# Three sums of the first groups moved into TensorE, and all order lists rewritten, in a gated linear attention with a maxout layer behind it

## The chip, the cores and the metric

The kernel runs on one core of one Trainium2 chip. A core has a matrix engine (TensorE, PE in the profile), VectorE (DVE), ScalarE (ACT), GpSimd (POOL), a queue engine that issues most transfers (SyncE, SP) and 16 DMA engines. The metric is the device time of one execution in microseconds (us); lower is better. Before the change three runs gave 565.18, 568.17 and 564.65 us; the median is 565.18.

## The reference

The first block is a recurrence with complex decays, for 4 batches x 8 heads, 768 steps, 48 dimensions:

```python
mag = np.sqrt(a_re * a_re + a_im * a_im)
scale = np.minimum(mag, 0.999) / (mag + 1e-06)
a_re_n, a_im_n = (a_re * scale, a_im * scale)
for t in range(S):
    ar, ai = (a_re_n[:, :, t, :, None], a_im_n[:, :, t, :, None])
    new_re = ar * S_re - ai * S_im
    new_im = ar * S_im + ai * S_re
    kv = np.einsum('bhd,bhe->bhde', k[:, :, t], v[:, :, t])
    S_re, S_im = (new_re + kv, new_im)
    y[:, :, t] = np.einsum('bhd,bhde->bhe', q[:, :, t], S_re)
```

Its output, as 3072 tokens of 384 features, goes through a maxout layer with weights in 64-bit floats (w1 to w3 of 384x768, w_out of 768x384):

```python
h = np.maximum(np.maximum(x @ w1, x @ w2), x @ w3)
return (h @ w_out).astype(np.float32)
```

## The kernel before

The steps are cut into 12 groups (numbers 0 to 11). A group is 128 steps of two batch entries, called x and y; six groups make one pair of batch entries. A decay is kept as the logarithm of its size and as an angle in turns, so that products of decays become sums over steps.

The order of all work is written out by hand as a long text, `SCHEDULE`, of words like `csx:0`: a step's name, x or y where it is done for one entry, and the group. A trailing 0 or 1 ahead of the colon (`lnw0:0`) means that only one half, x or y, is done. `run` (L952 ff.) turns a word into instructions; the helper class `Bound` chains the instructions of each engine, so each engine keeps the text's order strictly (all instructions therefore carry that helper's line, L209). `SLOTS` deals out the four double banks of PSUM in the order in which they are asked for. `OTHER` lists words that go to VectorE instead of their usual engine. Words that matter:

- `Lr`, `Li`, `Lk`, `Lq`, `Lv`: loads of a_re, a_im, k, q, v, issued on SP.
- `sqr sqi add lnL expw expe`: squares, their sum `L`, its logarithm, the size `w` and its inverse `e`. `relu` (tile `Ln`), `lne` (tile `e`) are the two parts of the logarithm of the decay; `Lnop` adds them: on VectorE in group 0, by an accumulating DMA from GpSimd's queue (`increase`, L254) in most later groups.
- `abs`, `pw` or `addw`: size plus |a_re|; in groups 0 and 1 (`SUMS`) it is summed by TensorE with the identity. `lnw expL mulw mulai stt atan`: the angle's half tangent and its arctangent in `w`. `half`: a_re's sign becomes a half turn in `ar`. `turn`: `w` = -w/pi + ar, on VectorE. `Cd`: the turns of the group before are added to `ar` by small DMAs.
- `cs` (L585 ff.): running sums of turns, by TensorE with the triangle `upto`. `t nf af sa sb`: fraction of a turn, sine and cosine.
- `sums`, `F` (L621 ff.): TensorE sums of `Ln` over ranges of steps, with 0/1 matrices (`mid`, `rest`, `cuts`); `En Ek Eq` and `f0` to `f3` are their exponentials on ScalarE. A factor tile `F` has the 48 dimensions twice, at partitions 0 and 64. `F` computes each head once, for one of the two places, and four instructions `f0` to `f3` write each result to both.
- `mk mq uk uq kEn`, `tpk tpq Kc Qc`, `Q1 Q2 QB KB QG`, `A B g0..g3 b0 b1`: rotated and scaled k and q, their transposes, the scores and their masked copy.
- `dk h0..h3`: the state; `y`, and its copy `x` (`xx`, `xy` in the lists): the attention output as features.
- `U..`/`u..`: up products and running maximum. Group 0 does them in halves (`U01x:0`), later groups whole (`U11:1`, 128x256 matmuls). `S P r o D`: the down product by a scheme with seven products, and the store.
- `WL Wa Wb Wc We Wf Wg`: 12 blocks of weights are loaded as 64-bit floats and turned into 32-bit ones by one ScalarE and four VectorE operations. `Wg` subtracts w1's block from that of w2 or w3, mostly by an accumulating DMA. `T t M m`: a product w1 @ w_out made once.
- `Zf`, `Zg`: zeros in the factor tiles' rows that `f0` to `f3` leave out, and in the state tiles.

Of the kernel before, what the change touches and what calls it, by code (L numbers as in the profile page):

```python
# [26 lines left out]
sqr:1 Wf9:0 half1:0 Lkx:0 csx:0 tx:0 nfx:0 mkx:0 sqi:1 atan1:0 add:1 turn1:0 afx:0 Wb10:0 sax:0 sbx:0 WL11:0 ukx:0
lnL:1 csy:0 Wc10:0 Eqy:0 Eky:0 expe:1 ty:0 Lqy:0 uqx:0 We10:0 Wf10:0 tpkx:0 kEnx:0 Wa11:0 Wb11:0 nfy:0 xor:1 tpqx:0
Qcx:0 T0:0 WL1:0 Wa1:0 Lky:0 Lvx:0 Wc11:0 f3x:0 f0x:0 Wb1:0 f2x:0 Q2x:0 We11:0 QBx:0 Kcx:0 relu:1 expw:1 abs:1
Wf11:0 half:1 Fy:0 f0y:0 T2:0 Lrx:2 lne:1 WL2:0 Lnop:1 Zg:0 pw:1 Wc1:0 Q1x:0 Lix:2 KBx:0 mky:0 t2:0 Lry:2 Ax:0  # L30
Wa2:0 We1:0 Wb2:0 t0:0 g0x:0 lnw:1 expL:1 Cdx:0 f2y:0 f1y:0 f3y:0 sqr:2 afy:0 Wf1:0 Wc2:0 say:0 sby:0 mulw:1
# [10 lines left out]
mqy:1 uqy:1 sumsx:2 Ekx:2 U22y:0 u22y:0 Oy:0 KBx:1 uky:1 tpky:1 sbx:2 afy:2 sax:2 Lkx:2 h0x:1 Eqx:2 mkx:2 h1x:1
h2x:1 Q1x:1 Enx:2 Lvy:1 tpqy:1 oy:0 Lqx:2 h3x:1 Qcy:1 Q2x:1 QBx:1 Ax:1 Kcy:1 QGx:1 Fx:2 f3x:2 Q1y:1 g0x:1 Q2y:1
sumsy:2 U22x:0 f1x:2 f2x:2 Lvx:2 g1x:1 g2x:1 g3x:1 Eqy:2 f0x:2 say:2 Ay:1 Bx:1 b0x:1 u22x:0 Lrx:3 Lry:3 Ox:0 kEny:1
KBy:1 sby:2 b1x:1 h0x:2 ukx:2 sqr:3 add:3 lnL:3 relu:3 expe:3 QBy:1 lne:3 Dy:0 g0y:1 Lnop:3 g1y:1 g2y:1 By:1 ox:0
g3y:1 b1y:1 Lky:2 Lqy:2 mqy:2 uqy:2 Eky:2 Eny:2 Liy:4 yx:1 xx:1 mqx:2 tpkx:2 uqx:2 expw:3 Kcx:2 mky:2 tpqx:2 dky:1
# [5 lines left out]
nfx:3 J4:0 afx:3 P7:1 Ay:2 sbx:3 ty:3 nfy:3 Lvx:3 g0y:2 g1y:2 g2y:2 Lry:4 sqr:4 By:2 sqi:4 add:4 sax:3 lnL:4 expe:4
Liy:5 Lix:5 g3y:2 ukx:3 uqx:3 P1:1 b0y:2 P6:1 dky:2 b1y:2 r1:1 h1y:2 QGy:2 h2y:2 Py:1 Lvy:3 Px:1 P4:1 h3y:2 xor:4
P5:1 lne:4 relu:4 yy:2 expw:4 abs:4 tpqx:3 r6:1 r5:1 r7:1 r57:1 oy:1 tpkx:3 xy:2 afy:3 P2:1 Lky:3 Qcx:3 S4:1 Kcx:3
P3:1 mky:3 half:4 Lnop:4 Fy:3 addw:4 f2y:3 f3y:3 f0y:3 f1y:3 kEnx:3 dkx:3 sumsx:4 ox:1 Lqy:3 mqy:3 Cdy:3 h0x:3
Q1x:3 QBx:3 h1x:3 lnw:4 h2x:3 Lqx:4 h3x:3 KBx:3 QGx:3 Q2x:3 Fx:4 Lkx:4 expL:4 Ekx:4 Eqx:4 mqx:4 say:3 sby:3 f1x:4
f2x:4 uqy:3 uky:3 U11:2 u11:2 U01:2 mulw:4 mulai:4 stt:4 f3x:4 mkx:4 Enx:4 u01:2 f0x:4 sqi:5 atan:4 Ax:3 g0x:3
g1x:3 Dy:1 Lry:5 g2x:3 h0y:3 Cdx:3 Bx:3 U02:2 g3x:3 turn:4 b0x:3 Lvy:4 u02:2 tpky:3 kEny:3 b1x:3 Kcy:3 tpqy:3 csx:4
Lrx:5 Qcy:3 tx:4 xor:5 csy:4 ty:4 nfy:4 sqr:5 add:5 Lqy:4 lnL:5 nfx:4 dky:3 relu:5 Q2y:3 sumsy:4 h1y:3 expe:5 afx:4
Eky:4 S3:2 h2y:3 h3y:3 yx:3 Eqy:4 Eny:4 KBy:3 Q1y:3 QBy:3 U12:2 Dx:1 u12:2 S1:2 expw:5 abs:5 addw:5 xx:3 P7:2 P1:2  # L60
sbx:4 half:5 sax:4 lne:5 Ay:3 g0y:3 By:3 Cdx:4 P5:2 r1:2 ukx:4 lnw:5 g1y:3 S2:2 S4:2 QGy:3 g2y:3 g3y:3 Py:2 Cdy:4
Lvx:4 h0x:4 P4:2 uqx:4 expL:5 afy:4 say:4 P6:2 b1y:3 Px:2 P2:2 P3:2 tpkx:4 r6:2 r5:2 r7:2 Liy:6 r57:2 tpqx:4
mulai:5 mqy:4 Lrx:6 b0y:3 yy:3 Kcx:4 KBx:4 Lix:6 sby:4 ox:2 mulw:5 Qcx:4 oy:2 stt:5 xy:3 Q1x:4 QBx:4 Lnop:5 sumsx:5
kEnx:4 Lky:4 mky:4 uky:4 QGx:4 Lry:6 Ekx:5 Fy:4 U01:3 U11:3 f0y:4 f1y:4 sqi:6 Enx:5 sqr:6 Lqx:5 u01:3 add:6 lnL:6
Q2x:4 relu:6 expe:6 u11:3 Lkx:5 Lvy:5 mkx:5 f2y:4 f3y:4 uqy:4 h0y:4 Eqx:5 mqx:5 U02:3 atan:5 dkx:4 u02:3 Fx:5 h1x:4
h2x:4 h3x:4 f0x:5 f1x:5 turn:5 Ax:4 g0x:4 g1x:4 g2x:4 g3x:4 f3x:5 f2x:5 xor:6 Bx:4 b1x:4 b0x:4 Dx:2 U12:3 u12:3
# [5 lines left out]
f3y:5 h0y:5 mulai:6 stt:6 QBx:5 u01:4 Eqx:6 U11:4 Q2x:5 half:6 Lrx:7 Enx:6 Ekx:6 tpky:5 tpqy:5 Qcy:5 u11:4 kEny:5
Lkx:6 Ax:5 sqi:7 atan:6 Kcy:5 mqx:6 mkx:6 g0x:5 Q2y:5 g1x:5 g2x:5 Bx:5 g3x:5 turn:6 b0x:5 Lvy:6 b1x:5 U02:4 u02:4
h0x:5 Lry:7 sqr:7 U12:4 add:7 lnL:7 u12:4 Fx:6 f2x:6 f0x:6 f3x:6 f1x:6 dkx:5 h1x:5 dky:5 sumsy:6 S3:4 csx:6 Eqy:6
Dx:3 h1y:5 KBy:5 Eny:6 expe:7 Lqy:6 mqy:6 Q1y:5 QBy:5 csy:6 ty:6 nfy:6 tx:6 relu:7 expw:7 nfx:6 P7:4 P1:4 Eky:6
lne:7 afx:6 By:5 yx:5 Ay:5 xor:7 S1:4 g0y:5 afy:6 P5:4 say:6 sbx:6 S2:4 g1y:5 g2y:5 xx:5 sax:6 uqx:6 g3y:5 Py:4
P4:4 r1:4 ukx:6 S4:4 P6:4 b1y:5 Dy:3 sby:6 b0y:5 Px:4 P2:4 P3:4 tpkx:6 abs:7 Kcx:6 tpqx:6 Lky:6 Qcx:6 QGy:5 r6:4
r5:4 r7:4 r57:4 ox:4 yy:5 xy:5 Lnop:7 sumsx:7 Fy:6 f0y:6 uqy:6 mky:6 uky:6 f2y:6 Lvx:6 Q1x:6 QBx:6 f3y:6 addw:7
lnw:7 Lix:8 U01:5 f1y:6 oy:4 kEnx:6 KBx:6 Ekx:7 u01:5 QGx:6 dkx:6 Lrx:8 Q2x:6 h1x:6 h2x:6 expL:7 Lry:8 Eqx:7 h3x:6
half:7 Lkx:7 mkx:7 Lqx:7 mulai:7 Ax:6 sqr:8 mulw:7 mqx:7 Cdy:6 stt:7 Cdx:6 U11:5 Liy:8 sqi:8 u11:5 atan:7 add:8  # L80
# [959 lines left out]
```

## Time and profile before

| | |
|---|---|
| median of 3 runs | 565.18 us |
| profiled execution | 564.54 us |
| its span (first to last instruction) | 562.9 us |
| mean granted TensorE clock | 0.981 |
| TensorE busy | 527.2 us (94%) |
| VectorE busy | 483.1 us (86%) |
| ScalarE busy | 393.6 us (70%), 73.1 of it in 57 table loads |
| GpSimd busy | 74.7 us (13%) |

The profile is one execution. Busy time counts an engine's instructions, not waits. `PE` is matmuls, `PEld` weight loads, which overlap them; each matmul in 32-bit floats leaves two records. A busy TensorE need not be at its peak. An arrow `<-` in brackets names what ended the idle time before an instruction. In the time lines a row's length may reach over the start of the next row, as instructions overlap a little; the distance from start to start is what an instruction costs its engine in a full queue.

### The profile page before, as it was taken

The numbers are of one execution on the slowest core, as the hardware profiler recorded it, in microseconds if no ns is written. First come the engines' busy times: TensorE is split into PE (matmuls) and PEld (weight loads), VectorE is DVE, ScalarE is ACT, GpSimd is POOL, SyncE is SP. The second block draws the span as 40 slices with busy tenths as digits, with TensorE's granted clock in tenths as the row PEclk, the third lists the DMA queues.
The fourth block names the chain that finished last, engine by engine and source line by source line (L and its number), as shares of the span: only waits on it lengthen the run. The fifth ranks groups of instructions, "written<-read, shape, count | busy, mean of one in ns | idle before, by whom it ended". The sixth has DMA issues, their size and how long they took to land.

```text
span 562.9 us, 22756 instructions
## 1 busy us (share of the span) xinstructions
PE 527.2 (94%) x10086; PEld 450.3 (80%) x10086; DVE 483.1 (86%) x762; ACT 393.6 (70%) x673; POOL 74.7 (13%) x115
## 2 busy tenths in 40 slices
PE   1579779989999999999999999999999999999997
PEld 0355578768888898888888988888888988998886
DVE  5996997999999998999897999989997799996423
ACT  6996986897679988775967776977787856631100
POOL 8304241002020020010002002002101102000000
PEclk9959899999999999999999999999999999999999
DMA  8987985463443432175353352352362233000000
GB/s 224 269 207 174 174 164 94 84 122 63 72 84 69 81 58 52 38 135 107 60 90 83 62 92 51 75 95 54 58 133 37 43 65 71 4 30 2 2 29 28
DMA packets 142097, 48.30 MB, mean 86 GB/s; under 512 B 130480, under 2 KB 135472, under 8 KB 142000
## 3 DMA queue, kind: packets, MB, share of 16 engines
q1 hardware_dynamic: 136128, 37.77, 31.5%
q0 software_dynamic: 5872, 9.08, 9.4%
q8 instruction: 79, 1.29, 0.9%
q14 instruction: 18, 0.15, 0.1%
HBM read 33.03 MB, written 4.72 MB: 67 GB/s over the span
## 4 chain that ended last, share of the span: by engine, by line
PE 74%; ACT 9%; DMA 6%; DVE 5%; issue 5%; SPq 1%; POOL 0%; ACTq 0%; DVEq 0%; POOLq 0%
PE up L209 29%; PE op L209 21%; PE y L209 6%; PE A L209 4%; PE tp L209 4%; PE dk L209 3%; PE cs L209 2%; PE sums L209 2%; DMA Ln<-e 2%; DMA w<-w 2%; PE F L209 1%; ACT L L209 1%; ACT xhx L209 1%; ACT e L209 1%; PE B L209 1%
## 5 line engine op out<-in xcount | busy, mean ns | idle before, releaser
L209 PE MATMUL up<-xhx,w 128*128 128x256 f32 x792 | 177.6, 382 | 0.2
L209 PEld LDWEIGHTS up<-xhx,w 128*128 128x128 f32 x792 | 148.4, 190 | 21.8 <-issue 0.9
L209 ACT ACT_TABLE_LOAD x57 | 73.1, 1283 | 1.8 <-PEq L1024 0.8
L209 POOL DMA_DIRECT2D ar<-nf x40 | 33.6, 1278 | 129.6 <-DVE ar L209 127.3
L209 PE MATMUL op<-wo,xhx 128*128 128x192 f32 (+1 forms) x220 | 49.0, 363 | 0.7 <-issue 0.5
L209 DVE TENSOR_TENSOR Q<-Q,f 112x1024 f32<-112x1024 f32 (+1 forms) x48 | 45.3, 952 | 0.4 <-ACT Q L209 0.4
L209 ACT COPY atm<-B 32x128 f32<-32x128 f32 x96 | 24.6, 256 | 28.4 <-PE B L209 14.8
L209 DVE TENSOR_TENSOR ot<-ot,op 128x192 f32<-128x192 f32 (+1 forms) x66 | 27.5, 418 | 15.4 <-PE op L209 8.7
L209 PEld LDWEIGHTS op<-wo,xhx 128*128 128x128 f32 x220 | 36.6, 190 | 5.0 <-issue 0.6
L209 PE MATMUL y<-atm,vb 128*32 128x64 f32 x1152 | 38.7, 221 | 0.0
L209 PE MATMUL y<-QG,g 112*32 112x64 f32 x1408 | 37.7, 219 | 0.6 <-ACT g L209 0.6
L209 ACT ACTIVATE f<-F 48x232 f32<-48x232 f32 x96 | 34.4, 359 | 3.5 <-PE F L209 1.6
L209 DVE TENSOR_TENSOR xhx<-xhx,up 128x768 f32<-128x768 f32 x22 | 21.0, 953 | 17.4 <-PE up L209 17.3
L209 PEld LDWEIGHTS y<-atm,vb 128*32 128x32 f32 x1152 | 32.1, 109 | 4.0 <-issue 2.3
L209 PEld LDWEIGHTS y<-QG,g 112*32 112x32 f32 x1408 | 34.6, 109 | 0.7 <-ACT g L209 0.7
L209 PE MATMUL op<-wo,strassen 128*128 128x192 f32 x176 | 33.0, 331 | 0.0
L209 ACT ACTIVATE xhx<-up 128x768 f32<-128x768 f32 x19 | 15.4, 809 | 25.1 <-PE up L209 25.1
L209 DVE COPY_PREDICATED atm<-masko,A 128x256 f32<-128x256 uint8 x72 | 31.3, 434 | 1.5
L209 PE MATMUL op<-w,strassen 128*128 128x192 f32 x176 | 32.4, 330 | 0.0
L209 PE MATMUL A<-Q,K 112*32 112x80 f32 x1536 | 31.4, 234 | 0.5 <-DVE Q L209 0.5
L209 PEld LDWEIGHTS A<-Q,K 112*32 112x32 f32 x1536 | 27.2, 110 | 4.7 <-issue 3.3
L209 POOL DMA_DIRECT2D Ln<-e x9 | 9.2, 1027 | 161.0 <-ACT e L209 112.9
(152 smaller groups left out, 1119.0 us busy)
## 6 DMA issues: line engine op xcount, KB each, us to landing
ar<-in_a_re_dram SPq DMA_DIRECT2D x24, 192.0 KB, 3.3
ai<-in_a_im_dram SPq DMA_DIRECT2D x24, 192.0 KB, 4.8
q<-in_q_dram SPq DMA_DIRECT2D x96, 48.0 KB, 2.7
k<-in_k_dram SPq DMA_DIRECT2D x96, 48.0 KB, 2.7
vb<-in_v_dram SPq DMA_DIRECT2D x96, 48.0 KB, 2.5
out_dram<-ot SPq DMA_DIRECT2D x24, 192.0 KB, 2.9
Ln<-e POOLq DMA_DIRECT2D x9, 384.0 KB, 4.2
w<-L POOLq DMA_DIRECT2D x9, 384.0 KB, 4.6
```

The source lines that it names most:

```text
L209: ins = f(*a, **kw)
```

## The change

Three sums of the first groups are left to TensorE's accumulation, and `SCHEDULE`, `SLOTS` and `OTHER` are replaced as a whole.

- Groups below `TURNS` = 2 have no `turn`: `cs` accumulates two products, `scaled` (the triangle times -1/pi) with the arctangents and `upto` with the half turns.
- Groups below `APART` = 2 have no `Lnop`: `sums` and `F` accumulate over `Ln` and over `e`. Group 0 keeps `e` in the place of the state tile `g3`, which is zeroed later (`Zh`); group 1 has a buffer of its own (`e+`).
- Groups below `WHOLE` = 3 compute `F` for both places, with 64 columns of weights, so one instruction `f0` takes the place of four. The tiles have 16 zero columns behind their end for the last head. `Zf` is gone.
- Group 0 keeps |a_re| in `L`, as the later groups do (`ADDS` is gone).

```diff
-    SUMS, ADDS = 2, 1
+    SUMS, TURNS, APART, WHOLE = 2, 2, 2, 3
...
+    scaled = const.tile([P, P], FP, name="scaled")
...
+        pool.tensor_single_scalar(out=scaled, in_=upto, scalar=-1.0 / math.pi, op=OP.mult)
...
         for nm in "Lwe":
-            once((nm, g), lambda: nat1.tile([P, W], FP, tag=nm, name=nm))
+            n = 16 if nm == "e" and g < APART else 0
+            if n and g == 0 and (nm, g) not in T:
+                T["e+", g] = gs[3].rearrange("p c i d -> p (c i d)")[:, 0:W + n]
+            once((nm + "+", g), lambda: nat1.tile([P, W + n], FP, tag=nm + "+" if n else nm, name=nm))
+            if n and (nm, g) not in T:
+                pool.memset(T["e+", g][:, W:], 0.0)
+            T[nm, g] = T[nm + "+", g][:, 0:W]
...
         elif name == "Lnop":
-            if g >= ADDS:
-                increase(part("Ln"), e)
-            else:
-                dve.scalar_tensor_tensor(out=part("Ln"), in0=L, scalar=-LNMAX, in1=e, op0=OP.add, op1=OP.add)
+            increase(part("Ln"), e)
...
+            parts = ((scaled, T["w", g]), (upto, flat(T["ar", g]))) if g < TURNS else ((upto, T["w", g]),)
             for ch in range(2):
-                for j in range(2):
-                    dst, m = ps[j * L64:(j + 1) * L64, ch * HC:(ch + 1) * HC], slice(ch * L64, (ch + 1) * L64)
-                    mm(out=dst, lhsT=upto[:, m], rhs=every(T["w", g][:, c * DM:(c + 1) * DM], j), start=True, stop=True)
+                for n, (mat, a) in enumerate(parts):
+                    for j in range(2):
+                        mm(out=ps[j * L64:(j + 1) * L64, ch * HC:(ch + 1) * HC], lhsT=mat[:, ch * L64:(ch + 1) * L64],
+                           rhs=every(a[:, c * DM:(c + 1) * DM], j), start=n == 0, stop=n == len(parts) - 1)
...
+                for t in ("Ln", "e")[0:2 if g < APART else 1]:
+                    for j in range(2):
+                        for ch in range(2):
+                            r = slice(ch * L64, (ch + 1) * L64)
+                            mm(out=ps[j * L64:(j + 1) * L64, ch, n * HC:(n + 1) * HC], lhsT=mat[r],
+                               rhs=every(T[t, g][r, c * DM:(c + 1) * DM], j), start=t == "Ln", stop=t == "e" or g >= APART)
...
+            for n in range(H):
+                i, j, u = n // 4, n // 2 % 2, n % 2
+                h = 2 * (2 * i + u) + j
+                at, m = (4 * i + 2 * u + j) * NF if g < WHOLE else (2 * i + j) * NF, c * DM + h * D
+                w = L64 if g < WHOLE else D
+                for t in ("Ln", "e")[0:2 if g < APART else 1]:
+                    for o in (0, L64) if g < WHOLE else (u * L64,):
                         for ch in range(2):
                             r = slice(ch * L64, (ch + 1) * L64)
+                            mm(out=ps[o:o + w, ch, at:at + NF], lhsT=T[t + "+", g][r, m:m + w], rhs=cuts[r],
+                               start=t == "Ln", stop=t == "e" or g >= APART)
...
+            if g < WHOLE:
+                activation(out=T["F", x][0:DD].rearrange("p (c s) j n -> p c (s j n)", c=2),
+                           in_=T["Fp", x][0:DD, :, 0:H * NF], func=AF.Exp, scale=-1.0)
...
+        elif name == "Zh":
+            pool.memset(gs[3][:, :, :, D:P - D], 0.0)
```

The words that leave the text are `Zf:0`, `Lnop0:0`, `Lnop1:0`, `Lnop:1`, `turn0:0`, `turn1:0`, `turn:1`, and `f1`, `f2`, `f3` of x and y in groups 0, 1 and 2; `Zh:0` comes in. All others are the same words in another order. From the stretch around the weight differences, before:

```
-Wg4:0 Wf5:0 u01x:0 Z3:0 WL7:0 addw:2 Wa7:0 Wg5:0 U11x:0 u11x:0 Eqy:1 QGy:0 dky:0 Eny:1 Lvx:1 h1y:0 By:0 h2y:0 Wb7:0
-h3y:0 b1y:0 half:2 U02x:0 Cdx:1 b0y:0 Wc7:0 Eky:1 lnw:2 yy:0 xy:0 U02y:0 Cdy:1 u02x:0 expL:2 mulai:2 sbx:1 mulw:2
-say:1 sby:1 We7:0 stt:2 atan:2 U01y:0 Wf7:0 U12x:0 sax:1 u12x:0 turn:2 U11y:0 u11y:0 Lky:1 u01y:0 WL8:0 Wa8:0 ukx:1
...
-dkx:2 xor:3 xy:1 Q1x:2 Enx:3 Eqx:3 abs:3 addw:3 h1x:2 h2x:2 Lqx:3 h3x:2 mqx:3 QGx:2 half:3 J3:0 h0y:2 U11:1 u11:1
```

and after:

```
+By:0 g2y:0 g3y:0 Z4:0 Wg4:0 b1y:0 U11x:0 b0y:0 yy:0 Wf5:0 Wa7:0 Lvy:2 u02x:0 h2y:0 u11x:0 addw:2 lnw:2 sumsy:1
+mkx:1 xy:0 half:2 U02y:0 Z3:0 mqx:1 Wb7:0 h3y:0 Wc7:0 expL:2 Eqy:1 Wg5:0 Cdx:1 mulai:2 Eky:1 Eny:1 say:1 WL8:0
+sbx:1 mulw:2 We7:0 stt:2 U12x:0 Wf7:0 U11y:0 sby:1 atan:2 u12x:0 Cdy:1 turn:2 Wg7:0 afx:1 sax:1 ukx:1 mqy:1 U01y:0
...
+QGx:2 uqy:2 Lky:3 Enx:3 Eky:3 Eny:3 Lqx:3 h0x:2 dkx:2 U11:1 u11:1 mky:3 h1x:2 h2x:2 h3x:2 QBx:2 Eqy:3 tpqy:2 Qcy:2
```

`OTHER` gives VectorE one `relu`, one `abs`, one `af`, one copy `x` and two of the copies `Kc`/`Qc` more than before (the words are others, too).

More of the change, by code (lines that the diff above doesn't have):

```diff
@@ L27 @@
[L27 to L31, printed above, removed]
@@ L42 @@
[L42 to L46, printed above, removed]
@@ L52 @@
[L52 to L66, printed above, removed]
@@ L72 @@
[L72 to L80, printed above, removed]
-lnL:8 relu:8 U12:5 u12:5 expe:8 Lvy:7 g0x:6 turn:7 g1x:6 U02:5 g2x:6 g3x:6 Bx:6 u02:5 lne:8 Enx:7 b1x:6 b0x:6
@@ new lines @@
+Ax:2 g0x:2 g1x:2 f1x:3 Dy:0 Lrx:4 Cdy:2 Bx:2 Lvy:3 g2x:2 Q1y:2 g3x:2 KBy:2 sqi:4 xor:4 sqr:4 add:4 QBy:2 Cdx:2
+atan:3 turn:3 b1x:2 U02:1 U12:1 u02:1 u12:1 lnL:4 b0x:2 relu:4 S3:1 S1:1 f3x:3 f2x:3 expe:4 lne:4 Lnop:4 yx:2 xx:2
+h0y:2 QGy:2 csx:3 mqx:3 csy:3 ty:3 nfy:3 expw:4 dky:2 abs:4 half:4 P7:1 h1y:2 addw:4 tx:3 nfx:3 P1:1 sbx:3 h2y:2
+h3y:2 afx:3 Ay:2 g0y:2 By:2 Px:1 g1y:2 g2y:2 g3y:2 r1:1 sax:3 uqx:3 Lqy:3 Liy:5 P5:1 b0y:2 S2:1 P2:1 S4:1 tpqx:3
+b1y:2 yy:2 ukx:3 Qcx:3 P6:1 P3:1 h0x:3 Dx:0 Q1x:3 J4:0 xy:2 Fy:3 f0y:3 Lkx:4 tpkx:3 Kcx:3 f1y:3 Py:1 f2y:3 P4:1
@@ new lines @@
+mqy:3 Cdx:3 QBx:3 r6:1 f3y:3 r5:1 afy:3 kEnx:3 r7:1 r57:1 lnw:4 expL:4 Fx:4 h0y:3 oy:1 sumsx:4 Ekx:4 Cdy:3 Eqx:4
+ox:1 QGx:3 dkx:3 h1x:3 h2x:3 U11:2 say:3 KBx:3 Lqx:4 h3x:3 sby:3 Enx:4 mqx:4 Q2x:3 f2x:4 f3x:4 f1x:4 Dy:1 U01:2
+f0x:4 uky:3 uqy:3 mulai:4 u11:2 Lrx:5 tpky:3 Kcy:3 tpqy:3 mulw:4 u01:2 stt:4 kEny:3 Bx:3 Lry:5 sqr:5 Lix:5 Ax:3
+g0x:3 sqi:5 g1x:3 g2x:3 g3x:3 Qcy:3 U02:2 add:5 b0x:3 b1x:3 yx:3 U12:2 xor:5 Q2y:3 Q1y:3 u02:2 QBy:3 S3:2 lnL:5
+KBy:3 relu:5 atan:4 expe:5 turn:4 Lrx:6 mkx:4 csx:4 tx:4 xx:3 u12:2 nfx:4 afx:4 S1:2 Lky:4 csy:4 ty:4 nfy:4 lne:5
@@ new lines @@
+Dx:1 sbx:4 sax:4 afy:4 Lnop:5 expw:5 abs:5 dky:3 sumsy:4 Eny:4 S2:2 Ay:3 g0y:3 g1y:3 h1y:3 P7:2 P1:2 P5:2 addw:5
+g2y:3 g3y:3 Eky:4 Eqy:4 h2y:3 By:3 QGy:3 P6:2 ukx:4 r1:2 r6:2 Py:2 P4:2 r5:2 r7:2 r57:2 b1y:3 b0y:3 yy:3 say:4
+sby:4 Lqy:4 Liy:6 h3y:3 uqx:4 oy:2 tpkx:4 Kcx:4 tpqx:4 Qcx:4 xy:3 S4:2 sumsx:5 kEnx:4 Enx:5 lnw:5 Q1x:4 QGx:4 Fy:4
+mky:4 mqy:4 uqy:4 Px:2 expL:5 Lry:6 U01:3 P2:2 u01:3 sqr:6 mulai:5 Lix:6 QBx:4 P3:2 U11:3 uky:4 mulw:5 stt:5 half:5
+sqi:6 f0y:4 xor:6 ox:2 h0x:4 Ekx:5 u11:3 Lkx:5 Eqx:5 Lvy:4 add:6 Lqx:5 mqx:5 U02:3 Q2x:4 u02:3 KBx:4 Lvx:4 Cdy:4
@@ new lines @@
+ukx:5 ox:3 Fy:5 Lix:7 b1y:4 Lqy:5 yy:4 tpkx:5 f2y:5 sby:5 Py:3 f3y:5 Kcx:5 Lky:5 mky:5 uky:5 f0y:5 xy:4 f1y:5 QBx:5
+P4:3 U01:4 u01:4 oy:3 KBx:5 Dx:3 kEnx:5 sumsx:6 mqy:5 lnw:6 expL:6 uqy:5 tpqy:5 Qcy:5 QGx:5 Q2x:5 Enx:6 Ekx:6
+tpky:5 kEny:5 half:6 Eqx:6 mulw:6 h0x:5 mulai:6 U11:4 Kcy:5 Q2y:5 Ax:5 stt:6 Lqx:6 g0x:5 mqx:6 u11:4 Lrx:7 Lry:7
+sqr:7 sqi:7 add:7 lnL:7 Lkx:6 g1x:5 g2x:5 atan:6 g3x:5 Bx:5 b1x:5 b0x:5 KBy:5 U02:4 Q1y:5 u02:4 Lvx:5 relu:7 U12:4
+Fx:6 f2x:6 f3x:6 f0x:6 f1x:6 turn:6 Dy:3 S3:4 dkx:5 sumsy:6 Eny:6 Eqy:6 u12:4 h1x:5 S1:4 mkx:6 csx:6 tx:6 nfx:6
@@ new lines @@
+Liy:8 Eky:6 xor:7 csy:6 Lqy:6 expe:7 h0y:5 afx:6 ty:6 P5:4 QBy:5 nfy:6 yx:5 xx:5 S2:4 lne:7 Lnop:7 expw:7 Ay:5
+g0y:5 g1y:5 g2y:5 afy:6 sbx:6 g3y:5 By:5 Lky:6 mky:6 abs:7 sax:6 b1y:5 QGy:5 b0y:5 P7:4 P1:4 Px:4 Py:4 P6:4 dky:5
+h1y:5 r1:4 Fy:6 Lrx:8 uqx:6 f2y:6 f0y:6 ukx:6 r6:4 r5:4 Lvx:6 f1y:6 r7:4 r57:4 f3y:6 P4:4 P2:4 yy:5 tpkx:6 oy:4
+tpqx:6 say:6 xy:5 addw:7 sby:6 U01:5 Kcx:6 Lry:8 Lix:8 S4:4 kEnx:6 sqr:8 Qcx:6 Q1x:6 QBx:6 uky:6 P3:4 KBx:6 u01:5
+sumsx:7 mqy:6 Eqx:7 Enx:7 Ekx:7 dkx:6 lnw:7 uqy:6 QGx:6 Q2x:6 half:7 U11:5 h1x:6 h2x:6 expL:7 h3x:6 mulai:7 Lky:7
@@ new lines @@
+Lkx:7 mulw:7 stt:7 u11:5 sqi:8 add:8 lnL:8 Lvy:6 Ax:6 g0x:6 g1x:6 expe:8 relu:8 Cdx:6 g2x:6 atan:7 Lqx:7 Bx:6 g3x:6
+U12:5 u12:5 b1x:6 b0x:6 U02:5 Fx:7 f0x:7 ox:4 f3x:7 mkx:7 mqx:7 Dx:4 tpky:6 Kcy:6 Cdy:6 turn:7 S3:5 u02:5 S1:5
+kEny:6 tpqy:6 Qcy:6 Q2y:6 sumsy:7 Eky:7 Q1y:6 QBy:6 Eny:7 Eqy:7 P7:5 f2x:7 csy:7 f1x:7 Dy:4 ty:7 nfy:7 csx:7 tx:7
+KBy:6 nfx:7 expw:8 Ay:6 g0y:6 dky:6 g1y:6 h1y:6 g2y:6 g3y:6 sbx:7 Fy:7 Liy:9 P5:5 afy:7 S2:5 h2y:6 h3y:6 afx:7
+mky:7 say:7 P1:5 Lrx:9 r1:5 yx:6 xx:6 sax:7 By:6 Lqy:7 mqy:7 P6:5 r6:5 Lvx:7 lne:8 Lnop:8 QGy:6 b0y:6 abs:8 addw:8
@@ new lines @@
+Lix:11 mulw:10 Eky:10 Dy:7 Q1y:9 Eqy:10 Fx:10 f1x:10 f3x:10 QBy:9 KBy:9 f0x:10 xx:9 Lrx:11 Lry:11 stt:10 sqr:11
+sqi:11 atan:10 add:11 lnL:11 relu:11 f2x:10 U12:8 U02:8 QGy:9 dky:9 u12:8 Cdy:9 Cdx:9 turn:10 expe:11 csx:10 tx:10
+csy:10 u02:8 S1:8 Lky:10 nfx:10 expw:11 Ay:9 P5:8 afx:10 lne:11 mqy:10 S2:8 P6:8 g0y:9 ty:10 g1y:9 sbx:10 sax:10
+S3:8 P1:8 r1:8 nfy:10 By:9 afy:10 g2y:9 h1y:9 say:10 g3y:9 sby:10 Lvx:10 b1y:9 h2y:9 h3y:9 r6:8 mky:10 b0y:9 Py:8
+P7:8 ukx:10 h0x:10 P4:8 r5:8 r7:8 Lnop:11 r57:8 uqx:10 yy:9 xy:9 tpkx:10 tpqx:10 Qcx:10 oy:8 S4:8 abs:11 Kcx:10
@@ L536, in gates @@
         elif name == "lne":
-            if g >= ADDS and "relu:%d" % g not in OTHER:
+            if "relu:%d" % g not in OTHER:
                 activation(out=e, in_=e, func=AF.Ln, scale=1e-6 * math.exp(-LNMAX), bias=least)
```

168 lines of the change are left out of this document (80 added, 88 removed).

## The prediction

> **What bounds the kernel now.** I read the page's slices first, then busy time in windows, then the chain that ended last, then the time lines of VectorE and TensorE around the places where the chain leaves an engine.
>
> The slices (each 14 us), with the granted clock:
>
> ```profile
> PE   1579779989999999999999999999999999999997
> DVE  5996997999999998999897999989997799996423
> PEclk9959899999999999999999999999999999999999
> ```
>
> TensorE is full from about slice 9 to the end; its idle time lies in the first nine. VectorE is full in the same first nine slices, except for two dips. Windows put sizes to it (columns: TensorE, its weight loads, VectorE, ScalarE and GpSimd busy, then clock, DMA share, GB/s):
>
> ```profile
> 20.00:30.00 10.00, 3.37 (x62) 2.45 (x54) 10.00 (x18) 9.85 (x16) 0.00 (x0) 0.82 0.97 282
> 30.00:40.00 10.00, 7.35 (x82) 5.36 (x79) 9.97 (x15) 9.88 (x17) 0.00 (x0) 0.50 0.84 197
> 50.00:60.00 10.00, 8.58 (x71) 4.66 (x69) 6.16 (x12) 8.60 (x13) 4.59 (x6) 1.00 0.64 147
> 80.00:90.00 10.00, 7.01 (x64) 6.71 (x64) 7.06 (x10) 5.84 (x10) 4.76 (x6) 1.00 0.80 141
> 128.00:550.00 422.00, 420.75 (x8183) 369.86 (x8183) 365.15 (x571) 285.10 (x481) 38.33 (x46) 1.00 0.33 63
> ```
>
> From 128 us on TensorE idles 1.3 of 422 us. So the end is the moment at which `U11:1`, the first full-width up product, starts, plus a fixed amount of matmul. That moment is 127.81 us; before it TensorE idles 31 us and runs at half clock from 27 to 43 us. The chain shows what else stands in front:
>
> ```profile
> 40.15 0.83 ACT e L209
> ...
> 41.29 10.03 DMA Ln<-e
> 51.34 0.84 ACT e L209
> ...
> 76.77 8.67 DMA w<-w
> ...
> 85.57 1.59 PE up L209 x12
> ```
>
> The first transfer is `Lnop:1`: group 1's decays are added by DMA, and ScalarE's `sqr:2` waits for the buffer `e` that the transfer reads. The second is `Wg5`, a weight difference that TensorE's `U12x:0` waits for. VectorE pays for both:
>
> ```profile
> 55.76 0.56 DVE L209 TENSOR_SCALAR xhx<-xhx 128x768 f32<-128x768 f32 x1 [3.47 <-ACT xhx L209]
> 87.19 0.42 DVE L209 TENSOR_TENSOR hT<-hT,up 128x256 f32<-128x256 f32 x1 [2.40 <-PE up L209]
> ```
>
> **What the parts cost.** Prices are start-to-start distances in the time lines. On TensorE:
>
> ```profile
> 92.25 0.56 PE L209 MATMUL F<-cuts,Ln 64*48 64x29 f32 x32
> 92.74 2.94 PE L209 MATMUL up<-xT,w 128*128 128x128 f32 x24
> ```
>
> One `F` (16 matmuls, 32 records) takes 0.49; the same way one `cs` takes 0.73 and one `sums` 0.81.
>
> - *Both parts of decays* (groups 0 and 1): `sums` doubles four times, 4 x 0.81 = 3.2 more on TensorE. Gone are two half-width `Lnop` on VectorE (2 x 0.47) and the transfer `Lnop:1`.
> - *Half turns* (groups 0 and 1): `cs` doubles four times, 2.9 more on TensorE. Gone are `turn0:0`, `turn1:0`, `turn:1` on VectorE, 0.47 + 0.47 + 0.87 = 1.8.
> - *Doubled factor rows* (groups 0 to 2): `F` does both halves of the partitions, and in groups 0 and 1 both decay parts too: four times 0.49 x 3, twice 0.49, 6.9 more on TensorE. Matmuls 64 wide instead of 48 are not in the trace for `F`; weight loads of 64 columns for `sums` take 137 ns against 124 for `F`, so the price lies between 6.9 and, with those loads in full, 8.2. I take 6.9, as loads overlap. On ScalarE 24 exponentials of 48x232 (0.36) become six of 112x464. That form is not in the trace: between 232 columns (0.36) and 768 (0.84) a line through 384 (0.49) gives 0.58. ScalarE saves 8.6 - 3.5 = 5.1.
> - *The choice list* moves ten operations net: VectorE gets 4.0 more (one `relu`, one `abs`, one `af`, one copy `x`, two copies K/Q at 1.14), ScalarE 4.2 less. In the new order ScalarE loads a table 54 times instead of 57, 3 x 1.28 = 3.8 less.
> - *GpSimd*: zeroing `g3` (`Zh`, 0.67) now waits for `F` of group 0, and the masks of `CL`, 10.6 us of work at 8.6 to 19.1 us before, queue behind it. `F` needs group 0's second `relu`, so I put its end at some 24 us and that of the masks at 35; the first user, `g0x:0`, ran at 45.4. Nothing, and up to 11 if that cover failed.
>
> Sums: TensorE +13.0, VectorE +1.2, ScalarE -13.1.
>
> **Where it lies.** I price every word and add up what stands ahead of a word in the order, before / after:
>
> | ahead of | VectorE | ScalarE | TensorE |
> |---|---|---|---|
> | `Wf5:0` | 61.9 / 59.3 | 59.2 / 57.1 | 36.4 / 51.5 |
> | `U12x:0` | 70.4 / 67.3 | 68.4 / 63.4 | 45.4 / 54.6 |
> | `xy:1` (last input of `U11:1`) | 108.6 / 108.6 | 101.6 / 94.5 | 86.2 / 98.6 |
> | `U11:1` | 114.0 / 111.1 | 103.4 / 96.0 | 86.2 / 99.6 |
> | the end | 469.3 / 470.5 | 374.8 / 361.6 | 510.3 / 523.3 |
>
> Behind `U11:1` stand 424.1 us of TensorE work before and 423.7 after: nothing won or lost there, if VectorE keeps ahead (its 355.3 becomes 359.4, still 64 less than TensorE's). Of the 13 added us, 9.2 stand ahead of `U12x:0`, where TensorE idles 18.6 us between 10 and 85.6; those are covered at full clock. The other 4.2 (`F` and `sums` of group 1's second half, `F` of group 2) stand between `U12x:0` and `U11:1`, where the trace idles only 2.2 in 42.2 us. They are on the path.
>
> So the gain is how much earlier `U12x:0` starts. `Wf5` ended at 76.4 in the trace with 62.8 of VectorE work done, 13.6 of lag. The wait of 3.47 goes: `sqr:2` writes another buffer than group 1's `e`. With 60.2 of work that gives 70.3; I add 1.5 for a wait that may take its place: 71.8. `Wg5` then lands some 7.5 later (6.8 is the median of these transfers, 8.67 this one): 79.3, against 85.57. Late next is TensorE itself, with 4.2 more to do. Start of `U11:1`: 6.3 - 4.2 = 2.1 earlier; with 0.4 less behind it, 2.5 in all. The profiled run took 564.54 (span 562.9 and 1.6 around it); 562.0 follows. The median of the three runs is 0.6 above the profiled one, so I say **562.5**.
>
> A row against the change: 32 records in 0.49 are 15 ns each, four quadrants of the array at once. If the wider matmuls kept only two quadrants going, an `F` record would cost 31 ns and `F` would add 6.9 more, 2.5 of it behind `U12x:0` (`F` of group 1's second half and of group 2): 564.5, a rival with 3 in 100. [...]
>
> **Rivals.**
>
> - *TensorE isn't the limit, VectorE is* (22 in 100). Both VectorE waits vanish, 3.47 + 2.40 = 5.9; with the same 108.6 of work ahead of `xy:1`, `U11:1` starts at 121.9: 558.6. It needs `U12x:0` by 75.5 (121.9 less 45.0 of work and 1.4 lost in between). For it: ScalarE has 7 less ahead of `xy:1`. Against: `Wf5` would have to end by 68.
> - *The transfer `Wg5` is as late as before* (13 in 100). It queues on GpSimd behind a transfer of group 2 (`addw:2`) and a memset, and DMA is 0.74 to 0.96 busy from 60 to 80 us. With `U12x:0` at 85.5, 4.2 more work and 0.4 less: **568.3**, slower. It decides from 81.8 on: a later start loses.
> - *TensorE is late itself* (11 in 100). The clock was 0.50 from 27 to 43 us, after gaps of 2.85 and 3.78. If it stays so, group 0's added 6.0 cost 12.0 and with group 1's 3.2 fill 15.2 of 18.6 idle us. If half of that idle is dependence that stays, `U12x:0` starts about 6 later than it did: 564.5 + 6 + 3.8 = 574. [...]
> - *The parts do nothing and only the order tells* (6 in 100): gains and losses cancel, 565.
>
> **How the numbers follow.** The forecast holds 45 in 100, with 560 to 565.5 of its own (`U12x:0` from 77 to 82.5). About 1% is what a measurement of this kernel can tell from no change: 559.5 and 570.8. Faster by more: most of the first rival (20) and the forecast's edge (5), 25. Slower: the late TensorE (10) and a few of the late transfer (3), 13. Within: 62. The range goes from 556 (first rival, 2.5 better) to 571; left out are the late TensorE and what lies under 556.
>
> **What would show it.** In the changed profile: no `Ln<-e` transfer near 41 to 51 us and no `sqr:2` wait; `f` as 112x464 at about 0.58, six times; two `F` groups of 128 records at about 2 us; the clock between 24 and 43 us; `up<-xT` behind `Wg5` at 77 to 82; `up<-xhx` starting at 123 to 127; TensorE full behind it. I am wrong if TensorE stalls after 130 us, if the masks hold up `g0x:0`, or if the new wide `F` takes far more than 2 us.

## The result, and the profile after

The changed kernel takes 568.20 us (median of 20 runs, 566.32 to 570.06) against 564.84 us before (20 runs, 559.29 to 568.17): a ratio of 1.0074, 95% interval 1.0052 to 1.0096. The change made the kernel 0.7% slower. The forecast was 562.5; the time lies inside the stated range, but the kernel moved the other way. The profiled execution took 568.71 us, span 567.0.

The slices of the changed kernel's page:

```profile
PE   3869999999999999999999999999999999999997
DVE  6899899899999998889889899999889898987314
PEclk9879999999999999999999999999999999999999
```

TensorE is full from the fourth slice on, not from the ninth, and the clock is back to full in the fourth (granted 1.00 from 40.0 us on). The windows (columns as in the prediction: TensorE, weight loads, VectorE, ScalarE, GpSimd busy, clock, DMA share, GB/s):

```profile
20.00:30.00 10.00, 7.93 (x143) 6.06 (x143) 7.18 (x13) 6.39 (x10) 0.69 (x3) 0.83 0.85 232
30.00:40.00 10.00, 5.66 (x46) 4.71 (x46) 9.96 (x15) 9.33 (x15) 9.35 (x13) 0.66 0.68 180
50.00:60.00 10.00, 9.75 (x243) 6.61 (x241) 10.00 (x16) 9.21 (x16) 5.67 (x7) 1.00 0.60 91
80.00:90.00 10.00, 9.39 (x152) 8.77 (x151) 9.61 (x15) 7.81 (x13) 2.62 (x3) 1.00 0.92 184
128.00:550.00 422.00, 420.26 (x8197) 367.06 (x8196) 365.24 (x571) 277.51 (x472) 38.12 (x46) 1.00 0.33 64
```

In the long window TensorE is busy 420.26 us where it was 420.75: by busy time nothing happened there. That is misleading, as will be seen. The chain that ended last, from the new kernel's page in order of time:

```profile
18.16 0.94 PE F L208 x55
19.10 2.12 issue
21.23 1.29 PE F L208 x73
...
58.45 2.04 PE F L208 x128
...
60.90 6.52 DMA xhx<-in_moe_w_dram
...
75.35 5.13 DMA w<-w
80.73 5.52 PE up L208 x48
...
92.83 2.00 PE F L208 x128
```

`Ln<-e` is gone from the chain, two of the wide `F` of 128 records take 2.0, `U12x:0` starts at 80.73 instead of 85.57. `U11:1` starts at 127.37 instead of 127.81. Its line before, and then after:

```profile
127.81 4.15 PE L209 MATMUL up<-xhx,w 128*128 128x256 f32 x18
```

```profile
126.30 1.14 PE L208 MATMUL dk<-vb,uk 64*64 64x48 f32 x64
127.37 4.15 PE L208 MATMUL up<-xhx,w 128*128 128x256 f32 x18
```

So the front won 0.44 us, and what stands behind `U11:1` took 567.0 - 127.37 = 439.6 instead of 562.9 - 127.81 = 435.1: 4.5 us lost in a stretch that the prediction had called unchanged. The number of matmuls of each kind there is the same but for 64 more short ones in `F` and a few fewer in `tp` and `sums`, which cancel. The loss is the question of this study.

### The profile page after: what moved, and what is told of

The parts are those of the page before. It is cut to its first block, busy times and chain, and to the rows that moved or that the text cites. A ratio compares the mean times of both kernels' runs of the same rounds, so it can differ in the third digit from the quotient of the medians.

```text
span 567.0 us, 23829 instructions
## 1 busy us (share of the span) xinstructions
PE 540.0 (95%) x10630; PEld 460.7 (81%) x10630; DVE 485.0 (86%) x763; ACT 379.9 (67%) x646; POOL 78.7 (14%) x118
## 4 chain that ended last, share of the span: by engine, by line
PE 89%; ACT 3%; DMA 3%; issue 2%; DVE 2%; POOL 0%; SPq 0%; DVEq 0%; ACTq 0%; POOLq 0%
PE up L208 33%; PE op L208 23%; PE y L208 7%; PE A L208 5%; PE tp L208 4%; PE dk L208 4%; PE cs L208 3%; PE F L208 3%; PE sums L208 2%; PE wm L208 2%; PE B L208 1%; DMA xhx<-in_moe_w_dram 1%; ACT L L208 1%; DMA w<-w 1%; DMA ai<-in_a_im_dram 1%
## 5 line engine op out<-in xcount | busy, mean ns | idle before, releaser
L208 ACT COPY atm<-B 32x128 f32<-32x128 f32 x96 | 24.5, 256 | 35.7 <-DVE atm L208 21.3
L208 DVE TENSOR_TENSOR Q<-Q,f 112x1024 f32<-112x1024 f32 (+1 forms) x48 | 45.4, 955 | 2.8 <-ACT Q L208 2.8
L208 ACT ACTIVATE f<-F 48x232 f32<-48x232 f32 (+1 forms) x78 | 29.2, 374 | 11.2 <-PE F L208 8.1
L208 PEld LDWEIGHTS op<-wo,strassen 128*128 128x128 f32 x176 | 28.8, 190 | 1.7 <-DVE strassen L208 0.5
```

The lines of the kernel that those rows point to most:

```text
L208: ins = f(*a, **kw)
```

## Experiments

Spans, starts of `U11:1` and the time behind it are of each run's profiled execution; medians are of its timed runs, ratios against runs of the kernel before on the same chip.

### Which half of the new order costs

The first two theories took the loss for a property of the order: R, that the new order of the words behind `U11:1` itself costs it; F, that the new front leaves something undone that is paid for behind it. Four kernels cross the front, the rest and the parts.

New front and parts, old order behind it:

```diff
 SCHEDULE = """
-(the changed kernel's words from U11:1 on)
+(before's words that the front has not done yet, in before's order)
```

> All three parts and the changed lists up to U11:1; behind it the words of the list before, with their banks and engines. Theory R (the rest of the new order costs, about 4 us behind U11:1, and the front wins nothing): the time is that of the kernel before, from -2 to +1 us, and behind U11:1 TensorE needs 431 to 432 us as before. Theory F (the front leaves a debt that is paid later: VectorE or ScalarE arrive at U11:1 with less done, and TensorE waits for them): about as slow as the changed kernel, +3 to +5 us, whatever list follows.

Measured: 589.39 us, 1.0479 (1.0429 to 1.0529) of before; behind `U11:1` 452.8 us.

Old front and code, new order behind it:

```diff
 SCHEDULE = """
-(before's words from U11:1 on)
+(the changed kernel's words that the front has not done yet, in its order)
```

> The code before without any of the parts and its list up to U11:1; behind it the words of the changed list. Theory R: +3 to +5 us against the kernel before, with 435 to 436 us behind U11:1. Theory F: the time of the kernel before, from -1 to +1 us.

Measured: 573.65 us, 1.0190 (1.0140 to 1.0239); behind `U11:1`, which starts at 132.6, 439.4 us. Nine words that the changed kernel does ahead of `U11:1` come on top of the old front here; two of them, `sumsy:3` and `tpky:2`, are TensorE's.

All parts in the old order (the words that they make needless are left out):

```diff
-    SUMS, ADDS = 2, 1
+    SUMS, TURNS, APART, WHOLE = 2, 2, 2, 3
 SCHEDULE = """
 (before's words in before's order)
```

> All three parts in the lists before: the words that the parts make needless are left out, Zh stands behind Zg, nothing else moves. If the parts are worth what my sum said, the wait of 3.5 us for Lnop:1 goes and 4 to 5 us of TensorE work come behind U12x:0: from -2 to +3 us against the kernel before, with U11:1 starting from 125 to 130 us. If the added matmuls are on the path as a whole, +13 us.

Measured: 598.55 us, 1.0648 (1.0592 to 1.0705); `U11:1` starts at 142.04, and behind it stand 453.6 us.

New order, no parts (before's code; the words that the parts had made needless stand where their inputs are ready):

```diff
-    SUMS, TURNS, APART, WHOLE = 2, 2, 2, 3
+    SUMS, ADDS = 2, 1
 SCHEDULE = """
 (the changed kernel's words in its order)
```

> The code before without the parts, in the changed lists; the left-out words (Lnop, turn, f1 to f3, Zf) stand where their inputs are ready. Theory R: 13 us less TensorE work than the changed kernel, but the front waits for Lnop:1 again and the rest of the order costs as it does there: +2 to +6 us against the kernel before. If the rest of the order costs nothing and only the parts do: -3 to +1 us.

Measured: 574.60 us, 1.0223 (1.0173 to 1.0273). Its profiled execution took 1342.8 us and can't be set beside the others.

All four times lie outside what was allowed for, and neither theory explains them. The old order behind `U11:1` takes 435 us in the kernel before, but 453 with the parts, word for word the same, and 453 behind the new front, with nine words fewer. The waits of TensorE tell what is new. Of the run with all parts in the old order, from 128 us on (us in total, times, longest; `U11:1` starts at 142.04 in it, so some of them stand ahead of it):

```profile
PE y L205 <- issue: 6.4, 6, 1.7
PE dk L205 <- issue: 5.9, 4, 1.6
PE B L205 <- issue: 2.6, 2, 1.6
PE up L205 <- issue: 2.1, 2, 1.1
PE sums L205 <- issue: 2.0, 2, 1.4
PE A L205 <- issue: 1.2, 2, 0.7
```

Before, in the same view:

```profile
PE op L209 <- issue: 0.5, 1, 0.5
PE F L209 <- issue: 0.3, 1, 0.3
```

`issue` is time in which the engine waited for nothing that the profile shows. The waits stand in the middle of a word, whose first matmuls had all they needed. In the time line of that run, the start is the first number and the duration the second:

```profile
335.44 1.01 PE L205 MATMUL dk<-vb,uk 64*64 64x48 f32 x52
337.81 0.43 PE L205 MATMUL dk<-vb,uk 64*64 64x48 f32 x12 [1.36 <-issue]
```

52 of 64 records run, then nothing for 1.4 us, then the other 12.

### TensorE's code comes in blocks

TensorE's instructions in a trace (matmuls, weight loads and some 150 others), numbered in order of start, put these stalls in one place. Behind `U11:1`, every start of a matmul that came over 0.2 us late was looked up:

| run | such stalls | at number 192 to 195, modulo 256 |
|---|---|---|
| before | 3 | 2 |
| after | 3 | 3 |
| new front, old rest | 16 | 14 |
| old front, new rest | 3 | 3 |
| parts in the old order | 17 | 17 |

And the transfers of code fit. Lines of the page's table of DMA queues (packets, MB, share), of before and then of after:

```profile
q8 instruction: 79, 1.29, 0.9%
```

```profile
q8 instruction: 83, 1.36, 1.0%
```

A packet of this queue is 16,384 bytes, 64 for each of 256 instructions; 79 x 256 = 20,224 and 83 x 256 = 21,248, where the traces hold 20,323 and 21,409 TensorE instructions. So each packet is one block of TensorE's code. In the stalls of the table at the borders, the matmul behind one starts 1.15 to 1.58 us after a packet has landed. Where the border before had stalled as well, the packet starts in most cases 1.1 to 1.4 us after that border. With about 1 us for the packet itself (a median of 0.99 before, 1.00 after) and some 1.4 behind it, that makes some 3.5 us from one border to the next. Over the whole stream 61 of the 79 packets before and 74 of the 83 after start behind the border of the same number (borders at number 192 modulo 256), the others up to 4.1 us ahead of it; the median is 0.84 and 0.88 us behind it. A block holds 128 matmul records and as many weight loads: short records of 13 to 20 ns run through in about 2 us, one `up` record takes 216 ns. How many blocks TensorE holds at a time, no run here shows.

From this came **theory B**: a block that has only short matmuls leaves TensorE waiting for the next one (it runs dry), and whether a run of short words fills a block depends on how many instructions stand ahead of it. The parts add 544 records, 1088 instructions, four blocks and 64. Played through with the starts of matmuls in the trace, blocks of 256 and 3.5 us from border to border at least, the rule gave no stall behind `U11:1` for before and after, 17 for the run with the parts in the old order. The rival, **theory N**, has the stalls made by the words' order or by other transfers. Each of the next four kernels only repeats the matmuls of one word ahead of `U12x:0`, writing the same values to the same place:

```diff
             ps = T["B", x] = banks("B")
-            for i in range(4):
+            for i in list(range(4)) * (3 if x == 0 else 1):
```

The 3 is 3, 5, 3 and 4. A round has 16 products, and each leaves two matmul records, so 64 instructions with the weight loads; the expectations call these records matmuls.

> The kernel before; in the word Bx:0 (ahead of U12x:0, where TensorE has 18 us to spare) the 32 matmuls are done three times over into the same places, so TensorE's stream holds 64 matmuls and 64 weight loads, 128 instructions, more, and everything behind them is the same work in the same order. Theory B (blocks): TensorE's code comes in blocks of 256 instructions, one transfer each, the next one asked for when a block is entered; a block whose 128 matmuls take less than some 3.5 us leaves TensorE without code. The order of before happens to put its runs of short matmuls across the borders of blocks; shifted by half a block they fall into one. Worked out from the matmul starts of before with that one rule: 22.8 to 24.5 us lost behind U11:1 at 19 or 20 borders, so some 458 us behind it instead of 435 and a median of 584 to 588. Theory N (the waits named issue are nothing of the code's place: the order of the words or the traffic of other transfers makes them): at most the 0.8 us of the added matmuls, hidden, so within 1% of before and 435 us behind U11:1.

Measured: 583.29 us, 1.0326 (1.0286 to 1.0367); behind `U11:1` 450.0 us, and the largest of TensorE's waits there are

```profile
PE y L209 <- issue: 3.2, 4, 1.1
PE dk L209 <- issue: 3.0, 4, 1.4
PE A L209 <- issue: 2.3, 3, 1.4
```

Of 17 late starts 16 are at number 192 to 195 modulo 256.

> As the run with half a block more, with the 32 matmuls of Bx:0 five times over: 256 instructions more, one whole block. Theory B: everything behind lies as in before against the borders of the blocks, so nothing is lost: 435 to 436 us behind U11:1, within 1% of before, although twice as many matmuls were added as in the other run. Theory N, or a theory by which the added matmuls themselves cost: at least as much as the run with half a block more.

Measured: 566.74 us, 1.0030 (0.9999 to 1.0061); behind `U11:1` 436.0 us.

> The changed kernel with 128 instructions more in Bx:0. Theory B: worked out from its own matmul starts, 12.9 to 14.8 us lost behind U11:1 at 13 borders and 2 to 3 us more ahead of it, part of them in idle time; so 452 to 455 us behind U11:1 instead of 439.6, a median of 581 to 586. Theory N: within 1% of the changed kernel, 568 us.

Measured: 588.89 us, 1.0424 (1.0378 to 1.0470); behind `U11:1` 451.1 us.

> The run of all parts in the order of before, which took 598.55 us and 453.6 us behind U11:1, with three more rounds of the 32 matmuls of Bx:0: 192 instructions, which with the 1088 that the parts add make 1280, five whole blocks, so that the words behind U11:1 lie against the borders as in before. Theory B: the 18 us lost behind U11:1 come back, 435 to 436 us behind it, a median of 578 to 583. Theory N: no gain, 598 to 600 us.

Measured: 578.75 us, 1.0250 (1.0213 to 1.0288), where the run without the repeats took 598.55; behind `U11:1` 434.2 us. More matmuls made the kernel 20 us faster. The wait at `dk` is gone; what is left of `issue` from 128 us on stands ahead of `U11:1`, which starts at 142.0:

```profile
PE y L205 <- issue: 0.9, 1, 0.9
PE F L205 <- issue: 0.8, 1, 0.8
```

Behind `U11:1` half a block costs 15 us in the one order and 11.5 in the other, twice as many matmuls that make a whole block cost 0.9. So theory B holds in all four as to where time is lost and where not, and theory N falls. Its sizes don't hold. Behind `U11:1` 14.9 us were lost where 22.8 to 24.5 were worked out, and 11.5 where it was 12.9 to 14.8; and the median of 588.89 lies above the range of 581 to 586, as `U11:1` starts 8.8 us later, at 136.2, and not 2 to 3. The 3.5 us are a typical sum and no lower bound: in the five runs with shifted borders (the first three kernels of the crossing and the two with half a block more) 50 blocks behind `U11:1` went through in 1.7 to 3.4 us.

The fifth kernel of this kind brings the new order without the parts back to the changed kernel's borders (the number is 2):

> The run of the new lists without the parts, which took 574.6 us, with the 32 matmuls of Bx:0 done twice: 64 instructions, so that the stream is 1024 instructions, four whole blocks, shorter than that of the changed kernel and its words lie against the borders as there. Theory B: by the changed kernel's matmul starts the shift costs 4.9 to 7.7 us behind U11:1; the runs with half a block more lost some 0.7 to 0.8 of what was worked out so, which makes 3.5 to 6 us to win back: 568.5 to 571. Theory N: 574 to 575. It also says what the parts themselves bring under the new lists: the changed kernel takes 568.2; if this run is above it, they bring the difference, if below, they cost it.

Measured: 577.33 us, 1.0226 (1.0181 to 1.0272). This missed: no gain against 574.60, which was 1.0223 of before. Which stalls that run had can't be told, as its profile is of no use. But two other profiles show why there was so little to win back. In the run with the old front and the new rest nearly all words behind `U11:1` lie 64 instructions off the changed kernel's borders, as in the run without the repeat, and it took 439.4 us behind `U11:1`, where the changed kernel took 439.6: this shift costs nothing there, where the rule had 4.9 to 7.7. The fifth kernel itself took 439.1 us behind `U11:1`, but it ran dry just ahead of it:

```profile
133.58 0.95 PE L207 MATMUL dk<-vb,uk 64*64 64x48 f32 x49
137.93 0.44 PE L207 MATMUL dk<-vb,uk 64*64 64x48 f32 x15 [3.40 <-issue]
138.30 5.84 PE L207 MATMUL up<-xhx,w 128*128 128x256 f32 x18
```

The 18 records of `U11:1` take 5.8 us there, not 4.1: from 139.4 us on the granted clock is 0.50 for 3.4 us.

### What is left: the order behind U11:1

Six profiles have few stalls behind `U11:1`. In them the time there goes by the order (late starts are of matmuls, over 0.2 us; all in us):

| kernel | order behind `U11:1` | `U11:1` at | behind it | of it late starts |
|---|---|---|---|---|
| before | old | 127.8 | 435.1 | 1.0 |
| before, one block more | old | 129.8 | 436.0 | 1.7 |
| parts in the old order, blocks back | old | 142.0 | 434.2 | 0 |
| after | new | 127.4 | 439.6 | 1.5 |
| old front, new rest | new | 132.6 | 439.4 | 2.5 |
| new order without parts, blocks back | new | 138.3 | 439.1 | 0.9, and 1.6 at half clock |

So theory R was right about this stretch after all, and the borders had hidden it. Without the last column the old order takes 434.1 to 434.3 us and the new one 436.6 to 438.1: the new order costs 2.3 to 4.0 us.

What in it? I split the time between the first and the last matmul behind `U11:1` by distances from start to start. Work is each record at the distance that it has among its own kind; changes are what the distance between unlike neighbours has above that; borders are what lies across a block's border.

| | before | after |
|---|---|---|
| first to last matmul | 431.1 | 435.3 |
| work | 411.0 | 411.0 |
| changes | 16.0 | 17.8 |
| borders | 1.5 | 2.9 |
| rest | 2.5 | 3.6 |

The work is equal, as forecast. Changes are between wide matmuls (`up`, `op`, `cs`) and narrow ones (the other words). The wide words behind `U11:1` are broken up by 51 groups of narrow ones before, by 61 after. In the profiles of the table a wide `up` record with a narrow one behind it takes 0.309, not 0.216; the last narrow one some 0.13 more than among its own; and the first wide one behind it 0.320, which the split above has under rest. Ten groups more at 0.09 + 0.13 + 0.10 are 3.2, and borders 1.4: the 4.3 us with 0.3 to spare. With the first wide record of each piece counted in, changes come to 16.5 to 16.8 us in the three profiles of the old order and to 20.0 to 20.5 in the three of the new. The borders' 1.4 belongs to these two profiles and not to the order, as the late starts in the table show. A time line of before shows it in whole words (TensorE; start, duration, then what was done):

```profile
179.36 0.48 PE L209 MATMUL B<-QB,KB 112*32 112x32 f32 x32
179.76 4.15 PE L209 MATMUL up<-xhx,w 128*128 128x256 f32 x18
183.85 0.66 PE L209 MATMUL tp<-ident,uk 64*112 64x64 f32 x16
...
533.75 15.70 PE L209 MATMUL up<-xhx,w 128*128 128x256 f32 x72
549.29 2.78 PE L209 MATMUL op<-wo,xhx 128*128 128x192 f32 x16
```

18 records between narrow words need 4.09 to the start of the next word; 72 in one piece need 15.54, which is 3.88 for 18.

Two kernels measure the price of a change by itself. In the middle of the full stretch both do 64 narrow and 64 wide products whose result the next matmuls write over, in one in turn, in the other in two runs:

```diff
+            if (g, f, i) == (4, 0, 1):
+                for n in range(64):
+                    narrow(n)
-                for n in range(64):
                     wide(n)
```

(With the second loop it is the version in two runs, without it the one in turn.) **Theory S** says that each change costs some 0.1 us, **theory P** that matmuls cost the same whatever stands beside them.

> The kernel before; ahead of the matmuls of U01:4 (in the middle of the stretch where TensorE is full) 128 matmuls whose result is written over at once: 64 narrow ones (64 rows, 64 columns, 29 wide, over the four quadrants as in F) and 64 wide ones (the first of U01:4, 256 wide), one of a kind after one of the other. 256 instructions, one whole block, so the words behind keep their place against the borders. Theory S (each change between narrow and wide costs TensorE some 0.1 us, which prices by the matmul leave out): a wide matmul with a narrow one behind it took 0.309 us from start to start in before, a narrow one with a wide one behind it 0.133 to 0.146, so 64 x 0.45 = 28.6 us, a median of 593. Theory P (matmuls cost what they cost in runs, whatever stands beside them): 64 x (0.219 + 0.015) = 15.0 us, a median of 579.7, as in the run with the same matmuls in two runs.

Measured: 619.48 us, 1.0978 (1.0936 to 1.1021).

> The same 128 matmuls at the same place, the 64 narrow ones first and then the 64 wide ones. Theory S and theory P: 15.0 us, a median of 579.7. What the two runs differ by is 126 changes between narrow and wide: 13.4 us by theory S, 0.1 us each, nothing by theory P.

Measured: 594.07 us, 1.0536 (1.0488 to 1.0583). The expectations forgot that each product leaves two records; both sums double, to 57.2 and 30.0 us above before. Measured were 55.0 and 29.6. The same matmuls cost 25.4 us more when they stand in turn, 0.2 for each of the 126 changes more. The time line of the version in turn:

```profile
252.81 0.30 PE L209 MATMUL up<-cuts,rest 64*64 64x29 f32 x2
253.03 0.70 PE L209 MATMUL up<-xhx,w 128*128 128x256 f32 x2
253.66 0.30 PE L209 MATMUL up<-cuts,rest 64*64 64x29 f32 x2
253.89 0.70 PE L209 MATMUL up<-xhx,w 128*128 128x256 f32 x2
```

One turn is 0.855 from start to start (252.81 to 253.66). In two runs, 128 narrow records take 2.00 and the wide ones 0.216 each, so one turn's four would be 0.463. (0.06 of the difference lies between the two narrow records of a turn, which start 0.079 apart, and 0.016 in a run.) Theory S holds, with a price of 0.39 a turn here, against 0.32 in the kernel's own words. What in the engine makes this price, no run here shows.

Last, an attempt to turn before's order into one with as many groups as the changed kernel's:

```diff
-... oy:1 tpkx:3 xy:2 afy:3 P2:1 Lky:3 ...
+... oy:1 P2:1 tpkx:3 xy:2 afy:3 Lky:3 ...
```

(one of twelve such moves, all of words `P`)

> The kernel before with twelve words P of the down product (1.3 us each, 0.69 us for half of one) moved one narrow word forward in the list behind U11:1, so that TensorE's words there stand in 63 groups of narrow words between wide ones and not in 51 (the changed kernel has 61); the code, the words ahead, and the number of instructions are unchanged, and by the block rule of the earlier runs no border loses anything. Theory S (changes between narrow and wide cost): a wide matmul with a narrow one behind it took 0.309 us in before and 0.219 in a run of wide ones, a narrow one with a wide one behind it 0.146 and 0.015: 0.22 us a group, 2.6 us for twelve; 437.7 us behind U11:1 instead of 434.2 to 436.0 with this list, a median some 0.5% above before. Theory P (what the groups are makes no difference; the new list behind U11:1 costs by something else): 434 to 436 us, no difference to before.

Measured: 573.08 us, 1.0151 (1.0100 to 1.0203), 444.5 us behind `U11:1`: 9.4 lost, not 2.6. Changes make 2.2 of it and the first wide matmuls 12 x 0.10 = 1.2, as theory S has it. The others are of the moves' own making: 2.1 at one border, where the rule saw none, and `op` words moved ahead that now wait,

```profile
PE op L207 <- issue: 2.1, 1, 2.1
PE op L207 <- ACT K L207: 1.1, 1, 1.1
PE op L207 <- DVE xhx L207: 0.7, 1, 0.7
```

so this run doesn't decide between S and P by its time. The last 1.6 are a stretch at half clock: the stall of 2.1 us ends at 415.74, the granted clock is 0.50 for 3.4 us from 415.7 on, and the `op` records there start 0.320 us apart, not 0.163. No kernel of this study is faster than the one before.

## Why the prediction was wrong

**The step that failed** is "Behind `U11:1` stand 424.1 us of TensorE work before and 423.7 after: nothing won or lost there, if VectorE keeps ahead". VectorE did keep ahead: no wait for it stands in that stretch. The work is equal too. But words priced one by one leave out what lies between them. The new order cuts the wide words with ten more groups of narrow ones, about 3 us by the split, and runs three times dry at a border of code blocks where before did so twice, 1.4 us more. By the split this is the whole loss. That the time still lies in the range is luck: the range was made of starts of `U11:1`, not of a loss behind it. The three waits of after, from 128 us on:

```profile
PE dk L208 <- issue: 0.9, 1, 0.9
PE B L208 <- issue: 0.3, 1, 0.3
PE A L208 <- issue: 0.3, 1, 0.3
```

The prediction had the view that warns of this: from 128 to 550 us TensorE is busy 420.75 of 422.00, but the records' busy time covers the slow starts (an `up` record lasts 0.38 us, and the next starts 0.216 behind it, or 0.309), and the work summed to 424.1 where the trace had 435.1 behind `U11:1`. Those 11 us had no owner in the sum, and were taken to stay as they were.

**The front** was to win 2.1 us by `U11:1`; it won 0.44. `U12x:0` started at 80.73, forecast 79.3, and from there `U11:1` took 46.6 (forecast 45.0 of work and 1.4). Two terms were off and half cancelled. `Wf5` ended at 75.1, not 71.8: the 3.47 wait went, as forecast, but between 20 us and `Wf5` VectorE waited 5.8 us in all, where before's 5.2 less 3.47 and the 1.5 allowed for make 3.3. The two longest, the first through `cs` and `nf`:

```profile
26.89 0.56 DVE L208 SCALAR_TENSOR_TENSOR nf<-t,cs 128x384 f32<-128x384 f32 x1 [2.82 <-ACT t L208]
...
68.41 0.56 DVE L208 TENSOR_SCALAR xhx<-xhx 128x768 f32<-128x768 f32 x1 [1.83 <-ACT xhx L208]
```

Ahead of the first the chain above has `F` of group 0: 55 records, 2.12 of `issue`, 73 records. It is a border again: the packet of code starts only at 18.30, 3.8 us after the border before, and lands at 19.64. An `F` of 128 records has as many instructions as a block; the three other ones of this length ran through without such a stall. The second comes from a weight block that landed at 67.4. The transfer `Wg5` then landed 5.4 us behind `Wf5`, not the 7.5 allowed.

**What held.** The parts' prices: the two `F` of 128 records in group 1 took 1.9 and 2.0 (those of group 0 took 2.35 and, with the stall, 4.35), the six exponentials of 112x464

```profile
L208 ACT ACTIVATE f<-F 112x464 f32<-112x464 f32 x6 | 3.3, 556 | 1.0 <-PE F L208 1.0
```

0.556, forecast 0.58 (the line through the prediction's own points gives 0.56 to 0.57). The wide `F` stayed at 15 ns a record, so that rival is out. Four quadrants at once fits the prices of 192 columns in before, too: 0.163 a record in `op` (128 rows, 128 columns of weights), 0.73 / 8 = 0.091 in `cs` (128x64), 0.81 / 16 = 0.051 in `sums` (64x64). The masks of `CL` ended at 45.4, against 35 forecast, and `KB` of VectorE waited 0.16 for them. The clock between 30 and 40 us rose from 0.50 to 0.66; what sets it, no run here shows. The late transfer was not the cause, and that its 568.3 is next to the measured time is chance: `U12x:0` started before 81.8. TensorE late itself, VectorE as the limit and the order alone did not come about. In single profiles the parts by themselves, with the repeats, start `U11:1` at 142.0, the new order by itself, with the repeat, at 138.3, and both together at 127.4. How much of that is the parts' own stays open, as the repeats put the borders right only behind `U11:1`: ahead of it `issue` waits at borders come to 5.9 and 5.8 us in the two, and to 2.9 in the changed kernel. By the medians the new order without the parts takes 1.022 of before and with them 1.007, so under the new order the parts bring some 8 us, stalls included.
